# Tables of powers made per half block beside the feed-forward part, d h kept on chip by rows of W1 units, and pools on two stacks

## The chip, the cores and the metric

The kernel runs on one core of one Trainium2 chip. The time is the device time of one execution in microseconds (us); quoted times are medians of several executions. Engines are named as the profile names them: PE (matmul), PEld (PE's weight loads), DVE (vector), ACT (scalar, with activation functions), POOL (GpSimd), SP (the queue that issues most DMAs). "Clock" is the mean share of full speed that the throttle granted PE.

## The reference

A state-space layer and a feed-forward layer, forward and backward, L = 2048 positions, D = 512 channels, N = 128 states, F = 1792 hidden units, bf16. Cut to what matters:

```python
def _A_ref(u, A_re, A_im, B_re, B_im, C_re, C_im, log_dt, Dskip):
    dt = jnp.exp(log_dt)[:, None]
    logdA = dt * (A_re + 1j * A_im)
    P = jnp.exp(logdA[:, :, None] * l[None, None, :])        # powers, D x N x L
    K = jnp.einsum("dn,dnl,dn->dl", Cc, P, dt * Bc).real     # the convolution's kernel
    y = irfft(rfft(pad(u)) * rfft(pad(K)))[:L]               # by FFT
    return y + u * Dskip
def _B_ref(x, w1, w2):
    return silu(x @ w1) @ w2
xn  = layernorm(x)
out = x + _A_ref(xn, ...) * silu(_B_ref(xn, w1, w2))
# returned: out and the gradients of x, A, B, C, log_dt, Dskip, w1, w2
```

The powers P are never stored. Each power of exp(dt A) is a product of one entry of a "high" and one of a "low" table; the tables are small, and outer products on DVE expand them. The 512 channels are done in 4 blocks of 128 channels, or 8 half blocks.

## The kernel before

The order of work, in one function:

```python
    half = gen_half(k)                        # tables of powers, 4 blocks, to DRAM (k.hd)
    ...
    interleave([half, gf], [1, 2])            # gf = gen_ffn_fwd(k): beside the feed-forward part
    run(gf)
    ...
        run(gen_ssm_fwd(k, 0))                # powers of block 0, with nothing beside them
        for b in range(1, NB):
            interleave([gen_ssm_fwd(k, b), gen_conv(k, b - 1)], [1, 2])
        run(gen_conv(k, NB - 1))
    with ... pools of the backward part:
        run(gen_dw2(k))                                        # with nothing beside it
        interleave([gen_ffn_bwd(k), gen_ssm_bwd(k)], [1, 2])   # d h and d x by chunks of 512 positions
        run(gen_dw1(k))
    with tc.tile_pool(name="fin", bufs=1) as k.fin:
        run(gen_ssm_final(k))                                  # gradients of A, B, C, log_dt
```

The end of a block's tables (`gen_half`, cut): scattered products on DVE, copies on POOL, and the store.

```python
        for c in range(2):
            tmul(nc, vXL[:, :, c, :, 1:8], sp(MG[:, 10:17]), sp(RC[:, c, 10:17]))
            ...
        for h in range(2):
            nc.gpsimd.tensor_copy(out=vXH[:, h, 0:2, :, :, 1], in_=vXH[:, h, 0:2, :, :, 0])        # L453
            nc.gpsimd.tensor_copy(out=vYL[...].rearrange(...), in_=vYL[...].rearrange(...))        # L454
            yh = T4[:, h, OYH:HSZ].rearrange("p (a u) -> p a u", u=2)
            nc.gpsimd.tensor_copy(out=yh[:, :, 1], in_=yh[:, :, 0])                                # L456
            nc.gpsimd.tensor_scalar(out=T4[:, h, OXH + 2048:OYL], in0=..., scalar1=-1.0, ...)      # L457
        nc.sync.dma_start(k.hd[:, 2 * b:2 * b + 2, :], T4[:])
```

The powers (`gen_ssm_fwd`, cut). X and YY are expanded tables. KF, a block's convolution kernel, is copied out of PSUM by ACT in an order that writes single bf16 elements 128 bytes apart.

```python
            for m, (ch, cl) in enumerate(((0, 0), (2, 1), (0, 1), (1, 0))):
                outer_mul(nc, X[:, m]..., H, ...)                        # DVE, four per step
            ...                                                          # pf_t: PE turns X; ACT evicts XTf
            ps = psum.tile([P, QCH, 2, 32], F32, name="ps_k", tag="ps")
            ...                                                          # ps_k: PE
            for e in range(2):
                es = slice(64 * e, 64 * e + 64)
                k.ev_k(KF[es, :, qb:qb + QCH].rearrange("p j q -> p q j"), ps[es, :, e, :])
```

In the backward part d h is computed in chunks of 512 positions, stored to DRAM as `dht_d`, and loaded again by 14 transposing DMAs for dW1:

```python
    nc.sync.dma_start(dhv[:, :, ls], dhT[:])                             # gen_ffn_bwd, once per chunk
    ...
    nc.sync.dma_start_transpose(out=DH[:, j], in_=k.dht_d[(f0 + j) * P:(f0 + j + 1) * P, :])   # gen_dw1
```

And the last line of the final part writes the gradient of log_dt, 512 bf16 values:

```python
        nc.sync.dma_start(k.outs[8].rearrange("(k p) -> p k", p=P), ddt_b[:])
```

Of the kernel before, what the change touches and what calls it, by code (L numbers as in the profile page):

```python
# [9 lines left out]
ALU = mybir.AluOpType  # L10
# [4 lines left out]
P = 128  # L15
# [136 lines left out]
def kernel(ctx, tc, A_u, A_A_re, A_A_im, A_B_re, A_B_im, A_C_re, A_C_im, A_log_dt, A_Dskip, B_x, B_w1, B_w2, grad_out,  # L152
# [6 lines left out]
    assert L == 2048 and N == 128 and D == 512 and F % P == 0  # L159
# [6 lines left out]
    k.const = ctx.enter_context(tc.tile_pool(name="const", bufs=1))  # L166
# [8 lines left out]
    k.xt_d = dr.tile([P, D // 2, 2, P], BF16, name="xt_d")  # L175
    k.yt_d = dr.tile([P, D // 4, 2, P], BF16, name="yt_d")
    k.hd = dr.tile([P, 2 * NB, HSZ], BF16, name="hd")
    k.s_d = dr.tile([NB, P, 512], F32, name="s_d")
    k.at_d = dr.tile([F, L], BF16, name="at_d")
    k.ut_d = dr.tile([F, L], BF16, name="ut_d")  # L180
    k.dht_d = dr.tile([F, L], BF16, name="dht_d")
    k.ident = make_identity(nc, k.const)
    k.xn = k.const.tile([P, T, D], BF16, name="xn")
    k.ev_c = Evac(nc, 0); k.ev_xt = Evac(nc, 0); k.ev_yt = Evac(nc, 0); k.ev_k = Evac(nc, 0); k.ev_w = Evac(nc, 2); k.ev_v = Evac(nc, 0)
    k.ev_x = Evac(nc, 2)

    with tc.tile_pool(name="lnp", bufs=1) as k.lnp:
        k.x_sb = k.lnp.tile([P, T, D], BF16, name="x_sb")
        for t0 in range(0, T, 4):
            nc.scalar.dma_start(k.x_sb[:, t0:t0 + 4, :], k.x_v[:, t0:t0 + 4, :])  # L190
        phase_setup(k)
        phase_ln(k)
    half = gen_half(k)
    hs = ExitStack()
    k.half = hs.enter_context(tc.tile_pool(name="half", bufs=1))
    next(half)

    k.fs = ExitStack()
    k.fp = k.fs.enter_context(tc.tile_pool(name="ffnf", bufs=1))
    load_ffn(k)  # L200
    gf = gen_ffn_fwd(k)
    interleave([half, gf], [1, 2])
    run(gf)
    k.fs.close()
    hs.close()
    k.K_b = {}
    with tc.tile_pool(name="kpool", bufs=2) as k.kpool, tc.tile_pool(name="cbig", bufs=1) as k.cbig, \
            tc.tile_pool(name="cio", bufs=1) as k.cio, tc.tile_pool(name="ssmf", bufs=2) as k.sp:
        k.K_ready = lambda b: None
        run(gen_ssm_fwd(k, 0))  # L210
        for b in range(1, NB):
            interleave([gen_ssm_fwd(k, b), gen_conv(k, b - 1)], [1, 2])
        run(gen_conv(k, NB - 1))
    with tc.tile_pool(name="ssmb", bufs=2) as k.bp, tc.tile_pool(name="ffnb", bufs=1) as k.fb:
        run(gen_dw2(k))
        interleave([gen_ffn_bwd(k), gen_ssm_bwd(k)], [1, 2])
        run(gen_dw1(k))
    with tc.tile_pool(name="fin", bufs=1) as k.fin:
        run(gen_ssm_final(k))


def load_ffn(k):
# [7 lines left out]
    for t0 in range(0, T, 4):  # L230
        for dk in range(0, DK, 2):
            pt = k.psumT.tile([P, 2, 4, P], BF16, name="pt_x", tag="pt")
            for i in range(2):
                for j in range(4):
                    nc.tensor.transpose(out=pt[:, i, j, :], in_=k.xn[:, t0 + j, (dk + i) * P:(dk + i + 1) * P], identity=k.ident[:])
            k.ev_x(k.XNT[:, dk:dk + 2, t0:t0 + 4, :], pt[:])


def phase_setup(k):
# [5 lines left out]
    k.ecst = const.tile([P, 24], F32, name="ecst")  # L245
    for m, e in enumerate(HEXPS):
        nc.gpsimd.memset(k.ecst[:, m:m + 1], e / (2.0 * math.pi))
    k.ones = const.tile([P, 1], BF16, name="ones"); nc.vector.memset(k.ones[:], 1.0)
    with k.tc.tile_pool(name="setup", bufs=1) as wk:
# [11 lines left out]
        TF = const.tile([P, 16, 2, P], BF16, name="TF")  # L261
# [3 lines left out]
        TI = const.tile([P, 16, 2, P], BF16, name="TI")  # L265
# [75 lines left out]

def phase_ln(k):
# [19 lines left out]

HEXPS = [1, 2, 3, 4, 5, 6, 7, 8, 16, 24] + [32 * i for i in range(1, 8)] + [256 * i for i in range(1, 8)]

OXL, OXH, OYL, OYH, HSZ = 0, 1024, 4096, 6144, 8192


def gen_half(k):

    nc, hp = k.nc, k.half  # L370
    D = k.D
    nat = {}
    for nm, key in (("Ar", "A_A_re"), ("Ai", "A_A_im"), ("Br", "A_B_re"), ("Bi", "A_B_im"), ("Cr", "A_C_re"), ("Ci", "A_C_im")):
        nat[nm] = hp.tile([P, 1, D], BF16, name="par_" + nm)
        nc.sync.dma_start_transpose(out=nat[nm][:], in_=k.ins[key])
    ldt = hp.tile([P, D], BF16, name="ldt")
    nc.sync.dma_start(ldt[:], k.ins["A_log_dt"].unsqueeze(0).to_broadcast([P, D]))
    T4 = hp.tile([P, 2, HSZ], BF16, name="T4")
    vXL = T4[:, :, OXL:OXH].rearrange("p h (c r l) -> p h c r l", c=2, l=8)
    vXH = T4[:, :, OXH:OYL].rearrange("p h (c r l u) -> p h c r l u", c=3, l=8, u=2)  # L380
    vYL = T4[:, :, OYL:OYH].rearrange("p h (c g y r l) -> p h c g y r l", c=2, y=2, r=4, l=8)
    vYH = T4[:, :, OYH:HSZ].rearrange("p h (c g y r m u) -> p h c g y r m u", c=2, y=2, r=4, m=4, u=2)
    for c in range(2):
        v = 1.0 - c
        nc.gpsimd.memset(vXL[:, :, c, :, 0], v)
        nc.gpsimd.memset(vXH[:, :, c, :, 0, 0], v)
        for h in range(2):
            nc.gpsimd.memset(vYL[:, h, c, :, 0, :, 0], v)
            nc.gpsimd.memset(vYH[:, h, c, :, 0, :, 0, 0], v)

    pr = lambda t: t.rearrange("p (b e q) -> p b q e", e=2, q=64)
    po = lambda t: t.rearrange("p (b q e) -> p b q e", e=2, q=64)
    scr = hp.tile([P, 6, D], F32, name="scr", tag="RC")
    dtb = hp.tile([P, D], BF16, name="dtb")
    nc.scalar.activation(out=dtb[:], in_=ldt[:], func=ACT.Exp)
    lamr = hp.tile([P, D], F32, name="lamr"); tau = hp.tile([P, D], F32, name="tau")
    Ctr = hp.tile([P, D], F32, name="Ctr"); Cti = hp.tile([P, D], F32, name="Cti")
    N_ = lambda nm: nat[nm][:, 0, :]
    nc.vector.tensor_tensor(out=po(lamr[:]), in0=pr(dtb[:]), in1=pr(N_("Ar")), op=ALU.mult)
    nc.vector.tensor_tensor(out=po(tau[:]), in0=pr(dtb[:]), in1=pr(N_("Ai")), op=ALU.mult)  # L400
# [5 lines left out]
    nc.vector.tensor_tensor(out=po(Ctr[:]), in0=pr(t1), in1=pr(t2), op=ALU.subtract)  # L406
    tmul(nc, t1, N_("Cr"), dBi)
    tmul(nc, t2, N_("Ci"), dBr)
    nc.vector.tensor_tensor(out=po(Cti[:]), in0=pr(t1), in1=pr(t2), op=ALU.add)
    yield  # L410
    for b in range(NB):
        ws = slice(b * P, b * P + P)
        MG = hp.tile([P, 24, P], F32, name="MG", tag="MG")
        RC = hp.tile([P, 2, 24, P], F32, name="RC", tag="RC")
        for m, e in enumerate(HEXPS):
            nc.scalar.activation(out=MG[:, m], in_=lamr[:, ws], func=ACT.Exp, scale=float(e))
        sh = [P, 24, P]
        tmul(nc, RC[:, 1], tau[:, ws].unsqueeze(1).to_broadcast(sh), k.ecst[:].unsqueeze(2).to_broadcast(sh))
        nc.vector.tensor_scalar(out=RC[:, 0], in0=RC[:, 1], scalar1=MAGIC, scalar2=MAGIC, op0=ALU.add, op1=ALU.subtract)
        nc.vector.tensor_tensor(out=RC[:, 1], in0=RC[:, 1], in1=RC[:, 0], op=ALU.subtract)  # L420
        yield
        nc.scalar.activation(out=RC[:, 0], in_=RC[:, 1], func=ACT.Abs)
        nc.scalar.activation(out=RC[:, 0], in_=RC[:, 0], func=ACT.Sin, scale=-2.0 * math.pi, bias=k.hpi[:])
        nc.scalar.activation(out=RC[:, 1, 0:10], in_=RC[:, 1, 0:10], func=ACT.Sin, scale=2.0 * math.pi)
        nc.scalar.activation(out=RC[:, 1, 10:24], in_=RC[:, 1, 10:24], func=ACT.Sin, scale=-2.0 * math.pi)
        yield
        sp = lambda t: t.rearrange("p m (h r) -> p h r m", h=2)
        for c in range(2):
            tmul(nc, vXL[:, :, c, :, 1:8], sp(MG[:, 10:17]), sp(RC[:, c, 10:17]))
            tmul(nc, vXH[:, :, c, :, 1:8, 0], sp(MG[:, 17:24]), sp(RC[:, c, 17:24]))  # L430
            for h in range(2):
                sy = lambda t: t[:, :, 64 * h:64 * h + 64].rearrange("p m (g r) -> p g r m", r=4)
                tmul(nc, vYL[:, h, c, :, 0, :, 1:8], sy(MG[:, 0:7]), sy(RC[:, c, 0:7]))
            tmul(nc, RC[:, c, 7:10], MG[:, 7:10], RC[:, c, 7:10])
        yield
        cb = lambda t: t[:, ws].unsqueeze(1).to_broadcast([P, 3, P])
        F = lambda c: RC[:, c, 7:10]
        g1, g2, Gr, Gi = RC[:, 0, 0:3], RC[:, 1, 0:3], RC[:, 0, 3:6], RC[:, 1, 3:6]
        tmul(nc, g1, F(0), cb(Ctr))
        tmul(nc, g2, F(1), cb(Cti))  # L440
        nc.vector.tensor_tensor(out=Gr, in0=g1, in1=g2, op=ALU.subtract)
        tmul(nc, g1, F(0), cb(Cti))
        tmul(nc, g2, F(1), cb(Ctr))
        nc.vector.tensor_tensor(out=Gi, in0=g1, in1=g2, op=ALU.add)
        for h in range(2):
            sy = lambda t: t[:, :, 64 * h:64 * h + 64].rearrange("p m (g r) -> p g r m", r=4)
            s1 = lambda t: t[:, b * P + 64 * h:b * P + 64 * h + 64].rearrange("p (g r) -> p g r", r=4)
            for c, (G_, C_) in enumerate(((Gr, Ctr), (Gi, Cti))):
                nc.scalar.copy(out=vYH[:, h, c, :, 0, :, 1:4, 0], in_=sy(F(c)))
                nc.scalar.copy(out=vYH[:, h, c, :, 1, :, 1:4, 0], in_=sy(G_))  # L450
# [413 lines left out]
```

## Time and profile before

The time was 1192.91 us, the median of 3 executions (1191.68 to 1198.79); a fourth, beside the first run of the changed kernel, makes the median 1195.09. The profiled execution spans 1186.1 us at a mean clock of 0.835.

Busy time of each engine over the whole span (part 1 of the page before), with the share of the span and the number of instructions:

```profile
PE 775.2 (65%) x6033; PEld 459.1 (39%) x6033; DVE 744.3 (63%) x1126; ACT 650.0 (55%) x1091; POOL 136.7 (12%) x96
```

No engine is near full, so the averages tell nothing of what to change. The windows view divides the span into stretches. Columns: from and to, the length, busy us of each engine with its number of instructions, the granted clock, the busy share of the DMA engines, GB/s. The cuts are at events of the program: the first feed-forward matmul (30), the first powers (310), the end of convolution 2 (695) and of convolution 3 (763), the first d h matmul (858), a cut in the last dW1 work (1109), after the last matmul (1171; the row of the last 15 us, without work on any engine, is left out).

```profile
core 0: us, PE busy (x) PEld busy (x) DVE busy (x) ACT busy (x) POOL busy (x), PEclk, DMA share, GB/s
0.00:30.00 30.00, 5.08 (x51) 4.37 (x52) 24.43 (x87) 13.66 (x13) 9.66 (x49) 1.00 0.62 201
30.00:310.00 280.00, 131.29 (x512) 50.77 (x511) 210.54 (x244) 160.50 (x319) 120.03 (x46) 0.73 0.40 145
310.00:695.00 385.00, 286.61 (x3612) 234.03 (x3613) 280.97 (x431) 330.82 (x500) 0.00 (x0) 0.86 0.48 150
695.00:763.00 68.00, 48.79 (x424) 34.02 (x421) 27.83 (x37) 52.54 (x93) 0.78 (x1) 0.87 0.19 47
763.00:858.00 95.00, 55.78 (x221) 22.47 (x222) 8.55 (x8) 4.09 (x7) 6.23 (x2) 0.82 0.97 222
858.00:1109.00 251.00, 196.75 (x965) 87.95 (x963) 162.61 (x271) 81.06 (x148) 0.00 (x0) 0.88 0.82 222
1109.00:1171.00 62.00, 50.91 (x256) 25.44 (x256) 29.35 (x48) 7.32 (x13) 0.00 (x0) 0.91 0.76 170
...
```

Read it by rows. In 30:310 (feed-forward and tables) PE is busy 131 of 280 us, and even DVE only 75%: engines wait for each other. In 310:695 (powers and convolutions 0 to 2) ACT is busy 331 of 385 us, 86%: it sets the pace. In 763:858 (dW2) DMA is busy 0.97 of the time and all engines are idle for much of it.

Who waited for whom in the feed-forward stretch, in the waits view of 30 to 310 (waiter <- what it waited for: us in total, number of times, longest):

```profile
POOL T_370 L454 <- DVE T_370 L60: 82.2, 3, 40.6
PE ps_h L478 <- ACT th L482: 76.8, 10, 35.5
DVE T_370 L60 <- DMA hd<-T_370: 38.2, 2, 22.9
...
ACT T_370 L449 <- DMA hd<-T_370: 21.3, 1, 21.3
```

PE waited 76.8 us for ACT to take its results out of PSUM, and in single waits of up to 35.5 us, far longer than any ACT instruction there. During that longest wait (167.3 to 202.8 us in the timeline) ACT stood for 21.3 us before a table instruction (L449), and the evictions that PE waited for ran only after it. So there is a chain from block to block: POOL waits for DVE, DVE and ACT wait for the store of the previous block's tables, and that store waits for POOL's copies, as the waits of the SP queue show:

```profile
SPq L458 <- POOL T_370 L456: 57.1, 4, 27.5
```

What those copies cost, from the groups of POOL (busy us, mean ns of one):

```profile
L454 POOL COPY T_370<-T_370 128x1024 bf16<-128x1024 bf16 x8 | 62.7, 7841 | 82.2 <-DVE T_370 L60 82.2
L457 POOL TENSOR_SCALAR T_370<-T_370 128x1024 bf16<-128x1024 bf16 x8 | 23.6, 2963 | 0.0
L453 POOL COPY T_370<-T_370 128x1024 bf16<-128x1024 bf16 x8 | 17.7, 2248 | 28.4 <-DVE T_370 L60 28.4
L456 POOL COPY T_370<-T_370 128x1024 bf16<-128x1024 bf16 x8 | 11.2, 1440 | 1.6 <-ACT T_370 L450 1.6
```

And two groups of part 5 of the page before: the KF eviction, with 1321 ns for 64x256 elements where 128x512 elements take 621, and one form of the feed-forward matmul.

```profile
L478 PE MATMUL ps_h<-XNT,W_403 128*128 128x512 bf16 x224 | 67.0, 451 | 102.9 <-ACT th L482 76.8
...
L74 ACT CAST KF<-ps_k 64x256 bf16<-64x256 f32 x64 | 84.6, 1321 | 4.1 <-PE ps_k L564 3.6
...
L74 ACT CAST XTf<-pf_t 128x512 bf16<-128x512 f32 x128 | 67.4, 621 | 17.3 <-PE pf_t L540 17.1
```

### The profile page before, as it was taken

How to read it: one execution, taken by the hardware profiler on the slowest of the kernel's cores; microseconds unless marked ns; L12 is line 12 of the kernel's file. 1: busy time of each engine (PE TensorE's matmuls, PEld its weight loads, DVE VectorE, ACT ScalarE, POOL GpSimd, SP SyncE). 2: the span in 40 equal slices, each digit the busy share in tenths (PEclk: the TensorE clock that was granted, in tenths of full speed). 3: DMA queues.
4: the chain of work that ended last, by engine and by line, in shares of the span. 5: the costliest groups of instructions: out<-in, count | busy, mean ns of one | idle time of the engine just before them, and what ended most of it. 6: DMA issues, size and time to landing. Idle time of an engine off the chain costs nothing. (4 is left out here: it accounts for less than half of the span.)

```text
span 1186.1 us, 15777 instructions
## 1 busy us (share of the span) xinstructions
PE 775.2 (65%) x6033; PEld 459.1 (39%) x6033; DVE 744.3 (63%) x1126; ACT 650.0 (55%) x1091; POOL 136.7 (12%) x96
## 2 busy tenths in 40 slices
PE   1462261367477777877777777546896886867693
PEld 1220020123266656656665654412342342423242
DVE  8788665896687759857965914600076575756153
ACT  4787362745177997999799797400042332323110
POOL 3229294360000000000000000200000000000000
PEclk9896675778777988899899888778998988988697
DMA  6221506538764513841651350499876889788981
GB/s 204 59 83 46 205 21 257 212 113 306 259 212 158 178 55 120 219 151 72 159 188 54 119 123 1 114 247 203 203 240 183 236 230 245 225 221 216 204 185 47
DMA packets 273262, 194.90 MB, mean 164 GB/s; under 512 B 189666, under 2 KB 250979, under 8 KB 271651
## 3 DMA queue, kind: packets, MB, share of 16 engines
q1 hardware_dynamic: 271842, 188.13, 55.0%
q0 software_dynamic: 768, 3.67, 0.9%
q10 hardware_dynamic: 576, 2.10, 0.6%
q8 instruction: 47, 0.77, 0.3%
q14 instruction: 29, 0.23, 0.1%
HBM read 84.28 MB, written 86.25 MB: 144 GB/s over the span
## 5 line engine op out<-in xcount | busy, mean ns | idle before, releaser
L74 ACT CAST Vb<-psV 128x512 bf16<-128x512 f32 x128 | 67.5, 595 | 124.5 <-PE psV L737 84.9
L478 PE MATMUL ps_h<-XNT,W_403 128*128 128x512 bf16 x224 | 67.0, 451 | 102.9 <-ACT th L482 76.8
L519 DVE TENSOR_TENSOR X<-H 128x1024 bf16<-128x1024 bf16 x128 | 83.8, 689 | 74.5 <-PE ps_k L564 64.6
L540 PE MATMUL pf_t<-ident_bfloat_80,X 128*128 128x128 bf16 x1024 | 93.8, 254 | 49.7 <-ACT KF L74 27.3
L540 PEld LDWEIGHTS <-X 128*128 128x128 bf16 x1024 | 80.3, 116 | 60.7 <-issue 52.6
L74 ACT CAST KF<-ps_k 64x256 bf16<-64x256 f32 x64 | 84.6, 1321 | 4.1 <-PE ps_k L564 3.6
L478 PEld LDWEIGHTS <-W_403 128*128 128x128 bf16 x224 | 23.7, 109 | 160.9 <-issue 144.4
L74 ACT CAST XTf<-pf_t 128x512 bf16<-128x512 f32 x128 | 67.4, 621 | 17.3 <-PE pf_t L540 17.1
L60 DVE TENSOR_TENSOR T_370<-MG,RC 128x896 bf16<-128x896 f32 (+1 forms) x32 | 49.2, 1615 | 43.0 <-DMA hd<-T_370 38.2
L737 PE MATMUL psV<-XT,Gbd 128*128 128x256 bf16 x256 | 48.1, 323 | 40.5 <-DMA XT<-xt_d 40.2
L454 POOL COPY T_370<-T_370 128x1024 bf16<-128x1024 bf16 x8 | 62.7, 7841 | 82.2 <-DVE T_370 L60 82.2
L713 POOL MEMSET Gbd<- 64x4096 bf16 x2 | 7.0, 3505 | 493.9 <-PE ps_i_7911 L130 493.9
L495 PE MATMUL ps_o<-W_405,aT 128*128 128x512 bf16 x224 | 57.2, 415 | 5.2 <-ACT th L482 5.2
L737 PEld LDWEIGHTS <-Gbd 128*128 128x128 bf16 x256 | 34.5, 178 | 64.9 <-DMA XT<-xt_d 30.4
L662 PE MATMUL ps_da<-DOT,W2T 128*128 128x512 bf16 x224 | 57.1, 400 | 0.2
L674 PE MATMUL ps_dx<-W1T,dhT 128*128 128x512 bf16 x224 | 56.3, 408 | 0.0
L632 PEld LDWEIGHTS <-A_ft 128*128 128x128 bf16 x224 | 22.7, 105 | 73.9 <-DMA A_ft<-at_d 28.7
L74 ACT COPY dftB<-pt_b 128x1024 bf16<-128x1024 bf16 x48 | 46.2, 1054 | 3.4 <-PE pt_b L95 3.3
L564 PE MATMUL ps_k<-YY,X 128*128 128x64 bf16 x1024 | 42.7, 203 | 7.1 <-ACT KF L74 6.6
L564 PEld LDWEIGHTS <-X 128*128 128x128 bf16 x1024 | 40.7, 105 | 9.8 <-issue 8.6
L95 PE MATMUL pt_b<-ident_bfloat_80,dftA 128*128 128x128 bf16 x384 | 31.8, 236 | 17.9 <-ACT dftB L74 10.7
L74 ACT COPY YTf<-pt_t 128x1024 bf16<-128x1024 bf16 x32 | 34.6, 1080 | 13.6 <-issue 8.5
(1576 smaller groups left out, 1932.3 us busy)
## 6 DMA issues: line engine op xcount, KB each, us to landing
hd<-T_370 SPq DMA_DIRECT2D x4, 4096.0 KB, 11.9
H<-hd SPq DMA_DIRECT2D x8, 2048.0 KB, 9.1
xt_d<-XTf SPq DMA_DIRECT2D x32, 512.0 KB, 3.1
XT<-xt_d SPq DMA_DIRECT2D x32, 512.0 KB, 4.5
YT<-yt_d SPq DMA_DIRECT2D x128, 128.0 KB, 4.5
yt_d<-YTf SPq DMA_DIRECT2D x32, 256.0 KB, 2.0
ut_d<-u SPq DMA_DIRECT2D x28, 256.0 KB, 2.4
at_d<-aT SPq DMA_DIRECT2D x4, 1792.0 KB, 6.8
```

The lines of the kernel that those rows point to most:

```text
L60: nc.vector.tensor_tensor(out=out, in0=a, in1=b, op=ALU.mult)
L74: self.nc.scalar.copy(out=out, in_=in_)
L95: nc.tensor.transpose(out=pt[:, gi, :], in_=A[:, c, g0 + gi, :, :].rearrange("p t e -> p (t e)"), identity=k.ident[:])
L454: nc.gpsimd.tensor_copy(out=vYL[:, h, :, :, 1].rearrange("p c g r l -> p c g (r l)"), in_=vYL[:, h, :, :, 0].rearrange("p c g r l -> p c g ...
L478: nc.tensor.matmul(out=ps[:], lhsT=W1[:, dk, ft * P:(ft + 1) * P], rhs=XNT[:, dk, 4 * tcn:4 * tcn + 4, :], start=(dk == 0), stop=(dk == DK ...
L495: nc.tensor.matmul(out=pso[:], lhsT=aT[:, ft, tt * P:(tt + 1) * P], rhs=W2[:, ft, :], start=(ft == 0), stop=(ft == FT - 1))
L519: nc.vector.tensor_tensor(out=out.rearrange("p (r h l u) -> p r h l u", h=nh, l=4, u=2), in0=h, in1=l, op=ALU.mult)
L540: nc.tensor.matmul(out=pf[:, qi, m // 2, :], lhsT=X[:, m, q + qi], rhs=k.ident[:], start=(m % 2 == 0), stop=(m % 2 == 1))
L564: nc.tensor.matmul(out=ps[:, q].rearrange("p e j -> p (e j)"), lhsT=X[:, m, q], rhs=YY[:, m // 2, q // 2, 1, 64 * (q % 2):64 * (q % 2) + 6 ...
L662: nc.tensor.matmul(out=ps[:], lhsT=W2T[:, dk, ft * P:(ft + 1) * P], rhs=DOT[:, dk, ls], start=(dk == 0), stop=(dk == DK - 1))
L674: nc.tensor.matmul(out=ps[:], lhsT=dhT[:, ft, tt * P:(tt + 1) * P], rhs=W1T[:, ft, :], start=(ft == 0), stop=(ft == FT - 1))
L737: nc.tensor.matmul(out=psV[:, qi].rearrange("p a b -> p (a b)"), lhsT=Gbd[:, :, :, :, 32 * (q_ // 2 % 2) + 4 * c + 2 * (q_ % 2) + q_ // 4] ...
```

## The change

The intent has four parts.

- **Tables on chip, per half block.** `half_angles` and `half_tables` make the tables of one half block (64 channels) in SBUF, right before they are used. The round trip through DRAM goes, POOL's copies go (a broadcast in the DVE product writes both copies), and 24 small Exps of a block become one for each half block.
- **Powers beside the feed-forward part.** `gen_ssm_fwd` is one generator for all half blocks, and 42 of its steps are issued between the steps of the feed-forward part. KF is evicted in an order that writes runs of eight elements.
- **Backward by rows of W1 units.** `gen_dh` takes 128 hidden units at a time, keeps d h in SBUF, turns it on PE, and does dW1 at once. d x comes last, with the last block's state-space backward (`gen_ssm_bwd`) and the final part, now in two parts (blocks 0 to 2, then block 3), beside it.
- **Pools.** Pools stand on two stacks ("left", "right") and release memory tile by tile, so that stages can overlap.

```diff
+    def pool(name, side, bufs=1):
+        return tc.tile_pool(name=name, bufs=bufs, side=side, reuse_waits="tile")
...
-    half = gen_half(k)
...
-    interleave([half, gf], [1, 2])
-    run(gf)
...
-        run(gen_ssm_fwd(k, 0))
-        for b in range(1, NB):
-            interleave([gen_ssm_fwd(k, b), gen_conv(k, b - 1)], [1, 2])
-        run(gen_conv(k, NB - 1))
-    with ... as k.bp, ... as k.fb:
-        run(gen_dw2(k))
-        interleave([gen_ffn_bwd(k), gen_ssm_bwd(k)], [1, 2])
-        run(gen_dw1(k))
-    with tc.tile_pool(name="fin", bufs=1) as k.fin:
-        run(gen_ssm_final(k))
+    gs = gen_ssm_fwd(k)
+    with pool("ffnf", "right") as k.fp:
+        load_ffn(k)
+        interleave([gen_ffn_fwd(k), BoundedGen(gs, 42)], [1, 1])
+    ...
+    for b in range(NB - 1):
+        upto(b)
+        interleave([BoundedGen(gs, 26), gen_conv(k, b)], [1, 2])
+    upto(NB - 1)
+    run(gs)
+    ...
+    gd = gen_dw2(k); gb = chain([gen_ssm_bwd(k, b) for b in range(NB - 1)])
+    interleave([gen_conv(k, NB - 1), BoundedGen(gb, 24)], [2, 1])
+    next(gd)
+    ...
+        with pool("ffnb", "right") as k.fb:
+            interleave([chain([gd, gen_dh(k)]), gb], [2, 1])
+        def final():
+            yield from gen_ssm_bwd(k, NB - 1)
+            for b0, nb in ((0, NB - 1), (NB - 1, 1)):
+                with pool("fin", "left") as k.fin:
+                    yield from gen_ssm_final(k, b0, nb)
+        with pool("dxp", "right", 2) as k.dp:
+            interleave([gen_dx(k), final()], [1, 3])
...
+def half_tables(k, w0):
+    tmul(nc, vXL[:, 0:2, :, 1:8], mg(10, 17), rc(10, 17))
+    for c in range(2):
+        tmul(nc, vXH[:, c, :, 1:8, :], mg(17, 24)[:, 0].unsqueeze(3).to_broadcast([P, 64, 7, 2]), rc(17, 24)[:, c]....)
...
-                k.ev_k(KF[es, :, qb:qb + QCH].rearrange("p j q -> p q j"), ps[es, :, e, :])
+                k.ev(KF[es, :, ql:ql + QCH], ps[es, :, e, :].rearrange("p q j -> p j q"))
+            if ql == 0 and hb + 1 < 2 * NB:
+                half_angles(k, 64 * (hb + 1))
...
+def gen_dh(k):
+    for ft in range(FT):
+        ...                                          # ps_da: PE; d h to k.dhT (SBUF): DVE
+            for j in range(8):
+                nc.tensor.transpose(out=pt[:, j, :], in_=k.dhT[:, ft, (t0 + j) * P:(t0 + j + 1) * P], identity=k.ident[:])
+            k.ev(DH[:, t0:t0 + 8, :], pt[:])
+        for t in range(T):
+            nc.tensor.matmul(out=ps[:], lhsT=DH[:, t, :], rhs=k.xn[:, t, :], start=(t == 0), stop=(t == T - 1))
```

## The prediction

> **What bounds the kernel now.** No single engine. The page gives PE 775 us, DVE 744, ACT 650 of a span of 1186. Busy times by stretch (windows view):
>
> | us | work | PE | DVE | ACT | POOL | DMA |
> |---|---|---|---|---|---|---|
> | 38-310 | FFN forward, tables | 125 | 204 | 156 | 118 | 0.41 |
> | 396-690 | powers 1-3, conv 0-2 | 224 | 214 | 268 | 0 | 0.43 |
> | 762-858 | dW2 | 56 | 9 | 5 | 7 | 0.96 |
> | 858-1105 | dh, dx, SSM backward | 195 | 160 | 81 | 0 | 0.82 |
> | 1105-1186 | dW1, final | 53 | 32 | 8 | 0 | 0.63 |
>
> The first is latency-bound (waits: PE 103 us on ACT; DVE 38 us on the table store; POOL copies of 7.8 us), the third ACT-bound, dW2 DMA-bound (A_ft transposes).
>
> **Removed.** The table round trip through DRAM (32 of 195 MB); 118 us of POOL; 96 small Exps (20 us of ACT) for 8 large ones; the d h round trip with 14 DMA transposes. YT loads: 128 become 64, in 2 KB runs.
>
> **Added.** Tables come in half width with more strided DVE work: about 18 us per half block (estimate from 2.08 us per 128x896 product), 148 us against 111. PE: 224 transposes of d h, 56 of dW1, about 31 us. ACT: 28 evictions of 1.05 us and, by the instruction order, 20 table loads against 14, 1.28 us each.
>
> **ACT.** KF evictions write single elements 128 B apart and took 1.31 us for 64x256. The Trainium skill, "ScalarE: Activation LUTs" (What ACT_TABLE_LOAD costs), gives 186 ns + 0.833 ns per element, so 0.40 us; 128x512 evictions (0.60) agree. The new order writes runs of eight but reads PSUM strided; I estimate 0.6 us: 64 x 0.7 = 45 us of ACT less. Totals: ACT about 647, DVE 785, PE 806.
>
> **New stages, from the busiest engine.**
> - Setup with parameters and first tables: 38 becomes 50.
> - FFN forward + 3.1 of 8 half blocks: ACT 200, PE 190, DVE 186; at 85%, 235.
> - conv 0-2 + 4.9 half blocks: ACT 280, DVE 277, PE 200; at 88%, 315.
> - conv 3 + SSM backward 0: PE 75, ACT 68: 80.
> - dW2, dh, dW1 + SSM backward 1-2: PE 56+57+53+31+40 = 238; about 255. DMA moves 43 MB, not limiting.
> - dx + SSM backward 3 + final: PE 76; 95 with the tail.
>
> Sum 1030; overlap across stages (pools released tile by tile) may give 15 back. About 170 us come off the critical path: 75 before conv 3, 95 after, where DMA-bound dW2 and dW1 get PE work beside them.
>
> **Predicted: 1015 us, 8 in 10 within 950 to 1080.** Faster by over 2%: 0.94; within 2%: 0.04; slower: 0.02.
>
> **Shown right by:** POOL near 20 us; about 150 MB moved; KF eviction at or below 0.7 us; FFN stretch with PE over 75%; conv stretch with DVE and ACT over 80%; no stretch with DMA over 0.9 and PE under 0.6. **Wrong** if KF stays at 1.3 us, or PE is below 85% in the d h stretch.
>
> **What would make it wrong.** In-order ACT, now fed by silu, evictions and tables, may stall the others: then the first two stretches run at 70% (1080). One buffer for T4, PC and DH may serialize halves.

## More of the kernel before

The mean of L454 hides two kinds. In POOL's timeline the first copy made for each of the four blocks is a long one: 22.2, 26.8 and 7.6 us (L454) and 7.0 us (L453). The other five copies of L454 took 1.03 to 1.43 us. Two of them, of one block (start us, us):

```profile
141.53 26.79 POOL L454 COPY T_370<-T_370 128x1024 bf16<-128x1024 bf16 x1 [23.97 <-DVE T_370 L60]
...
171.06 1.04 POOL L454 COPY T_370<-T_370 128x1024 bf16<-128x1024 bf16 x1
```

So the same copy need not take long on POOL. DVE was busy for over 99% of each long one (26.63 of 26.80 us in the one shown), but throughout some of the short ones too (1.26 and 1.03 us), so what held the long ones up is not shown. PE's wait of 35.5 us began as the copy of 26.79 us ended.

## The result, and the profile after

The changed kernel took **1029.72 us**, the median of 4 executions (1026.76 to 1033.08). Its ratio to the kernel before is 0.8617, with a 95% interval of 0.8576 to 0.8657. Here and below a ratio is the mean time of one kernel's fast runs over that of the other's of the same rounds, so it is not quite the ratio of the medians that are quoted. The profiled execution spans 1031.3 us at a clock of 0.894.

Part 1 of the page after:

```profile
PE 731.1 (71%) x6215; PEld 444.3 (43%) x6281; DVE 735.1 (71%) x1196; ACT 619.0 (60%) x1062; POOL 20.7 (2%) x85
```

PE's count is 66 below PEld's: some matmul records are missing from this trace, so that PE's busy time is a little too low. The windows view after, with the same columns and cuts at the same events (first feed-forward matmul 60, end of the feed-forward part 238, end of convolution 2 at 543 and of convolution 3 at 625, first d h matmul 710, first d x matmul 886, last matmul 970):

```profile
0.00:60.00 60.00, 11.79 (x98) 10.37 (x100) 48.17 (x126) 27.05 (x28) 13.67 (x83) 0.85 0.40 103
60.00:238.00 178.00, 149.64 (x1326) 85.54 (x1348) 162.31 (x261) 152.10 (x273) 0.00 (x0) 0.95 0.59 188
238.00:543.00 305.00, 222.01 (x2723) 174.59 (x2734) 258.40 (x375) 265.50 (x468) 7.01 (x2) 0.89 0.47 114
543.00:625.00 82.00, 61.81 (x540) 39.26 (x541) 48.22 (x63) 67.64 (x125) 0.00 (x0) 0.98 0.76 180
625.00:710.00 85.00, 60.62 (x255) 25.80 (x262) 15.40 (x18) 8.21 (x15) 0.00 (x0) 0.86 0.93 209
710.00:886.00 176.00, 151.89 (x924) 76.20 (x936) 107.82 (x135) 64.45 (x98) 0.00 (x0) 0.95 0.60 170
886.00:970.00 84.00, 73.37 (x355) 32.57 (x362) 65.99 (x137) 29.99 (x53) 0.00 (x0) 0.95 0.67 187
970.00:1031.00 61.00, 0.00 (x0) 0.00 (x0) 28.75 (x85) 4.05 (x7) 0.00 (x0) 0.53 0.12 28
```

Row against row, the two tables give where the time went (lengths in us, from the two windows views):

| stretch | before | after | difference |
|---|---|---|---|
| setup | 30 | 60 | +30 |
| feed-forward, tables; after: with about 3 of 8 half blocks of powers | 280 | 178 | -102 |
| the (other) powers, convolutions 0 to 2 | 385 | 305 | -80 |
| convolution 3 (after: with state-space backward 0) | 68 | 82 | +14 |
| dW2 | 95 | 85 | -10 |
| d h, d x, dW1, the rest of the state-space backward | 251 + 62 | 176 + 84 | -53 |
| after the last matmul | 15 | 61 | +46 |

So the front half, to the end of convolution 2, gave 152 us, and the back half only 3. Inside the back half 49 us were gained before the last matmul and 46 lost after it.

The waits of PE in the feed-forward stretch, in the waits view of 60 to 238 after, answer to those shown of before:

```profile
PE pf_t L532 <- ACT th L594: 6.0, 8, 2.0
...
PE ps_h L590 <- ACT th L594: 1.5, 4, 0.4
```

The long waits are gone: PE waits for ACT by 2.0 us at most where one wait had lasted 35.5. The feed-forward matmul in part 5 of the page after, and the KF eviction among ACT's groups by shape after:

```profile
L590 PE MATMUL ps_h<-XNT,W_408 128*128 128x512 bf16 x210 | 53.1, 389 | 2.6 <-ACT th L594 1.5
```

```profile
L74 ACT CAST KF<-ps_k 64x256 bf16<-64x256 f32 x64 | 24.9, 389 | 1.0 <-PE ps_k L556 0.5
```

KF went from 1321 to 389 ns. The feed-forward matmul went from 451 to 389 ns in the mean though nothing in it was changed. Its median is 380 ns before and 379 after, and single ones took up to 635; the granted clock of its stretch was 0.73 before and 0.95 after.

The end of the span after, in the timeline of the SP queue (start us, us, what is issued):

```profile
986.26 0.37 SPq L884 DMA_DIRECT2D out_dram<-ddt_b_10739  x1
...
989.58 4.00 SPq L822 DMA_DIRECT2D n_ldt_10758<-in_A_log_dt_dram  x1
999.98 1.73 SPq L850 DMA_DIRECT2D S_10803<-s_d  x4
...
1013.54 0.38 SPq L884 DMA_DIRECT2D out_dram<-ddt_b_10908  x1
```

The queue issues the first final part's write of 2-byte elements at 986.26, and the parameter loads of the second right behind it. The second part's state sums (S) are issued only at 999.98. The last write is issued at 1013.54, and the span ends at 1031.3. What these gaps were is in the chain of waits (start, us, link) of 970 to 1031, where the longest link is the first of these writes, and in the waits of the SP queue:

```profile
986.26 13.70 DMA out_dram<-ddt_b_10739
```

```profile
SPq L909 <- DMA out_dram<-ddt_b_10908: 16.1, 1, 16.1
...
SPq L850 <- DMA out_dram<-ddt_b_10739: 6.4, 1, 6.4
```

Of the 61 us, 13.7 went to a write of 768 bytes on which the loads of S waited, and 16.1 to one of 256 bytes at the very end.

### The profile page after: what moved, and what is told of

Its sections match the earlier page's. It is cut to its first block, busy times and chain, and to the rows that moved or that the text cites. A ratio compares the mean times of both kernels' runs of the same rounds, so it can differ in the third digit from the quotient of the medians.

```text
span 1031.3 us, 16058 instructions
## 1 busy us (share of the span) xinstructions
PE 731.1 (71%) x6215; PEld 444.3 (43%) x6281; DVE 735.1 (71%) x1196; ACT 619.0 (60%) x1062; POOL 20.7 (2%) x85
## 5 line engine op out<-in xcount | busy, mean ns | idle before, releaser
L506 DVE TENSOR_TENSOR X<-T_511 128x1024 bf16<-128x1024 bf16 x128 | 84.4, 704 | 14.7 <-PE ps_k L556 14.7
L532 PE MATMUL pf_t<-ident_bfloat_78,X 128*128 128x128 bf16 x1024 | 76.6, 230 | 22.9 <-DVE X L506 8.6
L532 PEld LDWEIGHTS <-X 128*128 128x128 bf16 x1024 | 67.9, 104 | 33.3 <-issue 17.2
L590 PE MATMUL ps_h<-XNT,W_408 128*128 128x512 bf16 x210 | 53.1, 389 | 2.6 <-ACT th L594 1.5
L60 DVE TENSOR_TENSOR T_511<-PC 128x896 bf16<-128x896 f32 (+1 forms) x40 | 51.7, 1348 | 0.4 <-ACT PC L452 0.4
L74 ACT COPY DH<-pt_dh 128x1024 bf16<-128x1024 bf16 x28 | 27.9, 1033 | 37.0 <-PE pt_dh L712 36.9
L680 PEld LDWEIGHTS <-A_ft 128*128 128x128 bf16 x224 | 23.0, 106 | 59.6 <-DMA A_ft<-at_d 30.1
L706 DVE SCALAR_TENSOR_TENSOR dhT<-th_ft,ps_da 128x512 bf16<-128x512 bf16 x56 | 35.6, 682 | 8.4 <-PE ps_da L705 8.2
L556 PEld LDWEIGHTS <-X 128*128 128x128 bf16 x1024 | 35.9, 100 | 6.1 <-issue 1.5
L87 PEld LDWEIGHTS <-TF 128*128 128x128 bf16 x384 | 28.1, 106 | 23.1 <-issue 21.7
L594 ACT ACTIVATE th<-ps_h 128x512 bf16<-128x512 f32 x56 | 37.8, 675 | 0.0
L593 ACT ACTIVATE aT<-ps_h 128x512 bf16<-128x512 f32 x56 | 37.4, 669 | 0.5 <-PE pf_t L532 0.3
```

Of the source, the lines that this page charges most:

```text
L60: nc.vector.tensor_tensor(out=out, in0=a, in1=b, op=ALU.mult)
L74: self.nc.scalar.copy(out=out, in_=in_)
L506: nc.vector.tensor_tensor(out=out.rearrange("p (r h l u) -> p r h l u", h=nh, l=4, u=2), in0=h, in1=l, op=ALU.mult)
L532: nc.tensor.matmul(out=pf[:, qi, m // 2, :], lhsT=X[:, m, q + qi], rhs=k.ident[:], start=(m % 2 == 0), stop=(m % 2 == 1))
L556: nc.tensor.matmul(out=ps[:, q].rearrange("p e j -> p (e j)"), lhsT=X[:, m, q], rhs=YY[:, m // 2, q // 2, 1, 64 * (q % 2):64 * (q % 2) + 6 ...
L590: nc.tensor.matmul(out=ps[:], lhsT=W1[:, dk, ft * P:(ft + 1) * P], rhs=XNT[:, dk, 4 * tcn:4 * tcn + 4, :], start=(dk == 0), stop=(dk == DK ...
```

## The experiments

All twelve kernels gave correct results. The eight named t1 to t4 and f1 to f4 ran on one chip, where the kernel before had a median of 1197.5 us, the four named e1 to e4 on another, where it took 1194.7 us. The changed kernel itself was timed in neither group, so differences against its 1029.72 us may cross chips; the ratio to the kernel before, from the same chip in each case, is the safer number and is given each time. The changed kernel's ratio is 0.8617.

### Front half: is it the overlap?

Theory OVERLAP: the 152 us of the front half come from powers that now run beside the feed-forward part. Rival TABLES: they come from cheaper tables, whatever runs beside them. f1 keeps the new tables and runs the 42 steps after the feed-forward part.

```diff
-        interleave([gen_ffn_fwd(k), BoundedGen(gs, 42)], [1, 1])
+        run(gen_ffn_fwd(k))
+        run(BoundedGen(gs, 42))
```

> Changed kernel with the feed-forward forward run to its end first, and the same 42 steps of powers and tables after it. In the changed kernel both together took 178 us (60 to 238) at PE 150, DVE 162, ACT 152 busy. Theory OVERLAP: the gain ahead of conv 3 (152 us, where 75 were predicted) comes from running the two beside each other. Alone, the FFN takes about 120 us (PE 107 us busy) and three half blocks at DVE 43 us each about 135: 255 together, so the run takes 65 to 85 us more, 1095 to 1115. Rival TABLES: it is the new making of tables (no POOL, no store to DRAM) that freed the FFN; then running apart costs under 35 us, below 1065.

Measured: 1072.24 us, ratio 0.8954 (0.8933 to 0.8976), so 43 us more than the changed kernel. This lies between the two theories. The windows view of f1, feed-forward part and then the 42 steps:

```profile
60.00:172.00 112.00, 105.73 (x485) 45.10 (x493) 60.74 (x115) 84.39 (x157) 0.00 (x0) 1.00 0.63 207
172.00:268.00 96.00, 55.28 (x834) 48.79 (x830) 95.68 (x142) 66.01 (x112) 0.00 (x0) 0.74 0.46 130
```

Alone, the feed-forward part is bound by PE (106 of 112 us, clock 1.00), and the powers are bound by DVE (95.7 of 96 us). They need different engines, and so they fit into one another: 208 us apart, 178 together, 30 us; by the end of convolution 2 f1 is 40 us behind. (The profiled execution of f1 was its slowest, 1081.66 us and so 9 above its median, so these two are a little high.) The two parts were not wholly apart even here, since the first half block was ready 19 us after the feed-forward part and each further one took 38.4 us. So overlap is worth 43 us and, as an estimate from these two numbers, at most some 19 more: between 28% and 41% of the 152.

### Front half: the KF eviction

Theory ACT: where ACT sets the pace, the 0.93 us saved in each of 64 KF evictions come off the time. Rival: other engines fill the gap. f2 puts the old order into the changed kernel, f3 the new order alone into the kernel before.

```diff
 (f2, in the kernel after)
-                k.ev(KF[es, :, ql:ql + QCH], ps[es, :, e, :].rearrange("p q j -> p j q"))
+                k.ev(KF[es, :, ql:ql + QCH].rearrange("p j q -> p q j"), ps[es, :, e, :])
 (f3, in the kernel before)
-                k.ev_k(KF[es, :, qb:qb + QCH].rearrange("p j q -> p q j"), ps[es, :, e, :])
+                k.ev_k(KF[es, :, qb:qb + QCH], ps[es, :, e, :].rearrange("p q j -> p j q"))
```

> Changed kernel with the KF evictions written as before, single elements 64 B apart, instead of runs of eight. They take 0.39 us each now and took 1.32 before: 60 us of ACT more over 64. Theory ACT: ACT is 265 of 305 us busy in the conv stretch and 152 of 178 in the FFN stretch, so it becomes the limit of both: 35 to 55 us more, 1065 to 1085. Rival SLACK: DVE (258 of 305, 162 of 178) sets the pace and ACT fills its gaps: at most 15 us more.

> The kernel before with only the order of the KF eviction changed. ACT was 331 of 385 us busy from 310 to 695. Theory ACT: 60 us of ACT less there; the next limits are PE 287 and DVE 281, so 35 to 55 us less: 1140 to 1160. Rival SLACK: under 15 us less.

Measured: f2 1076.07 us, ratio 0.8976 (0.8937 to 0.9015), 46 us more than the changed kernel. f3 1146.74 us, ratio 0.9586 (0.9554 to 0.9618), 51 us less than before on the same chip. The KF groups of f2 and of f3:

```profile
L74 ACT CAST KF<-ps_k 64x256 bf16<-64x256 f32 x64 | 83.7, 1307 | 0.5
```

```profile
L74 ACT CAST KF<-ps_k 64x256 bf16<-64x256 f32 x64 | 24.8, 387 | 2.1 <-PE ps_k L564 1.7
```

One line is worth 46 to 51 us in either kernel, against 59 us of ACT time saved (83.7 - 24.9): theory ACT holds. The duration itself agrees with the Trainium skill, "ScalarE: Activation LUTs" (What ACT_TABLE_LOAD costs): 186 ns + 0.833 ns x 256 is 399 ns, and the traces show 387 and 389. That the old order costs 3.4 times as much fits the note on 16-byte cachelines in "SBUF — State Buffer" (Door 1: The DMA port swizzle), by which each access that crosses to a new line pays a penalty: the old order wrote every element 128 bytes from the last (64 in f2, whose KF tile is half as wide), the new one runs of eight bf16, 16 bytes. The runs show the two durations; that the cacheline is the reason was not tested: the edit changes the order of the reads from PSUM together with that of the writes.

### Front half: the copies on POOL

Theory POOL: in the kernel before, POOL's copies stood in the chain of the tables and so in front of ACT and PE. Rival: moved to DVE, the busiest engine of the stretch, they cost as much there. f4 moves the four copies, nothing else, in the kernel before.

```diff
-            nc.gpsimd.tensor_copy(out=vXH[:, h, 0:2, :, :, 1], in_=vXH[:, h, 0:2, :, :, 0])
+            nc.vector.tensor_copy(out=vXH[:, h, 0:2, :, :, 1], in_=vXH[:, h, 0:2, :, :, 0])
 (the other three alike)
```

> The kernel before with the copies of the tables on DVE instead of POOL. The FFN stretch took 280 us; POOL was 118 us busy in it with copies of 7.8 us, DVE 204. On DVE the copies should cost about 25 us (an estimate from 0.7 us for 1024 elements written whole[...]). Theory POOL: the tables wait for POOL and with them the store, DVE and the in-order ACT; the stretch gets 30 to 60 us shorter, 1135 to 1165 us. Rival CHAIN: the stretch is held by ACT and DVE waiting on each other and on the store of one table tile with a single buffer, which stays: within 15 us of 1195.

Measured: 1153.3 us, ratio 0.9629 (0.9608 to 0.9651), 44 us less than before. Groups of DVE in f4:

```profile
L60 DVE TENSOR_TENSOR T<-MG,RC 128x896 bf16<-128x896 f32 x16 | 32.9, 2055 | 7.5 <-ACT RC L423 7.5
...
L454 DVE COPY T<-T 128x1024 bf16<-128x1024 bf16 x8 | 3.3, 415 | 0.0
```

On DVE all four copies cost 18.4 us together, on POOL 115 us (62.7 + 23.6 + 17.7 + 11.2): the copy of L454 takes 415 ns on DVE; on POOL it took 7841 in the mean and 1384 in the median. The feed-forward stretch shrank from 280 to 237 us, in the windows view of f4:

```profile
30.00:267.00 237.00, 137.07 (x501) 52.44 (x508) 204.22 (x276) 160.14 (x319) 5.57 (x13) 0.76 0.47 171
```

Theory POOL holds: the copies' place on POOL cost the time. Why the first copy of each block took so long on POOL, f4 cannot tell, since it takes all of them away. The first line of DVE's groups settles a side question: the product of 128x896 takes 2055 ns without POOL, as before with it (2081), so its 1471 ns in the changed kernel comes from the new layout and not from a quiet POOL.

Together: KF 46 to 51, POOL 44, overlap 43 are 133 to 138 of the 152 us. The three need not add exactly, each being measured in a kernel of its own. The rest, some 15, is the sum of several untested terms: no table round trip through DRAM, fewer small Exps, and against them 30 us of later start.

### Back half: what does the end of the span wait for?

Two theories for the tail. MEMORY: the second final part's loads of S go into memory that the first part's tiles still hold, and these are held until the 13.7 us write of ddt_b has landed. LOADS: the second part waits for its own parameter loads (ACT waited 12.6 us for n_ldt, DVE then 12.1 for ACT), which are issued too late. t1 loads the parameters of both parts early, into a pool of their own; t2 leaves the loads and has PE turn ddt_b, so that the write is in rows.

```diff
 (t1)
+            with pool("finp", "left") as fpar:
+                par = {b0: load_final(k, b0, nb, fpar) for b0, nb in ((0, NB - 1), (NB - 1, 1))}
                 yield from gen_ssm_bwd(k, NB - 1)
...
+                        yield from gen_ssm_final(k, b0, nb, par[b0])
 (t2)
-        nc.sync.dma_start(k.outs[8][bs].rearrange("(k p) -> p k", p=P), ddt_b[:])
+    pt = k.psumT.tile([DK, P], BF16, name="pt_ddt", tag="pt")
+    nc.tensor.transpose(out=pt[:], in_=ddt_b[:], identity=k.ident[:])
+    row = fin.tile([DK, P], BF16, name="ddt_row" + sfx)
+    nc.vector.tensor_copy(out=row[:], in_=pt[:])
+    nc.sync.dma_start(k.outs[8][bs].rearrange("(k p) -> k p", p=P), row[:])
```

> Changed kernel with the parameter loads of both final parts made early, in a pool of their own. Changed kernel: 1029.7 us. Theory LOADS: the 12.1 us that DVE waited before the second final part are the late parameter loads (put into the queue at 986.7, log dt landed at about 1000), so this run ends 10 to 13 us earlier, about 1018. Theory MEMORY: the loads of S for block 3 wait anyway until the slow write of the first ddt (986.3 to 1000.0) has left the memory that they reuse, so only the products of parameters (2 us) come off: 1025 to 1029. Theory DVE: DVE is 97% busy from 960 to 990 and sets the end; 1025 or later.

> Changed kernel with both ddt results turned into rows by PE before they are written (256 B runs instead of single 2-byte elements); nothing else. MEMORY: the first write no longer holds the reload of S (12 us), and the last write takes 2 us instead of 16: together 24 to 28 us less, 1002 to 1006. LOADS: only the last write shrinks, 14 us: about 1016. DVE: at most 14 us too.

Measured: t1 1027.74 us, ratio 0.8588 (0.8555 to 0.8621): 2 us, inside the noise. The S loads still came late, and the SP queue still waited for the write before them; the waits views of t1 from 960 on:

```profile
DVE cm L60 <- DMA S<-s_d: 11.6, 2, 9.2
...
SPq L860 <- DMA out_dram<-ddt_b: 9.0, 1, 9.0
```

t2 1009.47 us, ratio 0.8421 (0.8397 to 0.8445): 20 us less. Here S is loaded right behind the parameters, in the timeline of the SP queue of t2:

```profile
994.05 7.69 SPq L850 DMA_DIRECT2D S<-s_d  x16
```

MEMORY holds, and LOADS falls as the main cause: with the parameters early nothing was won, with the write short 20 us were. But most of the 20 is the last write, which LOADS allowed too: from its issue to the end of the span 17.8 us became 2.4. The first write's part is the smaller one, since the last is issued only 5.5 us sooner (1008.03 against 1013.54); MEMORY had put the whole at 24 to 28. What sets the pace there in t2, by its chain of waits, is the SP queue, which issues the parameter and S loads one by one from 990.5 to 1001.7 us. The late parameters were in part the write's doing as well: the load of log_dt's last 128 elements, issued right behind the write, held ACT up for 12.6 us in the changed kernel and for 4.4 in t2. "DMA: Bandwidth & Descriptors" (Specifications) gives 512 bytes as the least transfer at line rate and a read-modify-write below that. This does not tell the two writes apart: the rows of t2 have 256 bytes, and the last landed within 2.4 us. The traces show 13.7 us for 384 single elements and 16.1 for 128; why they take so long was not tested.

t3 does all of it: rows, parameters early, and the final part of blocks 0 to 2 ahead of the last state-space backward, so that only block 3 is left at the end.

```diff
                 with pool("fin", "left") as k.fin:
-                    yield from gen_ssm_final(k, b0, nb)
+                    yield from gen_ssm_final(k, 0, NB - 1, par[0])
+                yield from gen_ssm_bwd(k, NB - 1)
+                with pool("fin", "left") as k.fin:
+                    yield from gen_ssm_final(k, NB - 1, 1, par[NB - 1])
```

> Rows for ddt, parameters early, and the final part of blocks 0 to 2 put ahead of the backward of block 3, so that only the small final part of block 3 is left after it. If the tail is latency of a chain that could run beside d x, the end comes near the end of the d x work on DVE (989): 990 to 998 us, 33 to 40 us less than the changed kernel. Theory DVE: moving it only crowds DVE in the d x stretch; no better than the run with rows alone (over 1003).

Measured: 994.66 us, ratio 0.831 (0.8291 to 0.8329): 35 us less than the changed kernel and 15 less than rows alone; how the 15 divide between the early parameters (2 us by themselves, in t1) and the new order was not separated. The stretch from the first d x matmul to the end went from 145 to 108 us, against 95 in the prediction.

### Back half: dW2 and d h

dW2 was to have PE work beside it. In the changed kernel d h follows dW2 in one chain, and only the state-space backward is beside it: PE is busy 61 us of 85, 5 us more than in the dW2 stretch before, with DMA at 0.93. t4 runs two steps of dW2 and then the rest of it between steps of d h.

```diff
-            interleave([chain([gd, gen_dh(k)]), gb], [2, 1])
+            next(gd); next(gd)
+            interleave([gd, gen_dh(k), gb], [1, 3, 3])
```

> Changed kernel, but after two dW2 steps the rest of dW2 runs mixed with the d h steps instead of ahead of them. Theory DMA: the dW2 stretch (85 us, DMA share 0.93, PE 61 us busy, 30 us of waits for A_ft) is bound by the transposing loads; spread over the 261 us of both stretches (PE 212 busy) they hide, and the run takes 15 to 25 us less: 1005 to 1015. Rival ORDER: the in-order queue of loads delays a_ft, th_ft and XT behind the transposes as much as it hides; within 8 us of 1029.7.

Measured: 994.56 us, ratio 0.8305 (0.8279 to 0.8332): 35 us less, more than expected. dW2, d h and dW1 together took 224 us instead of 261; the windows view of t4:

```profile
622.00:700.00 78.00, 61.78 (x340) 29.43 (x348) 35.11 (x41) 17.60 (x27) 0.00 (x0) 0.93 0.95 241
700.00:846.00 146.00, 139.13 (x833) 70.41 (x846) 87.75 (x111) 54.00 (x86) 0.00 (x0) 0.98 0.75 195
```

The second stretch has PE busy 95% of the time. The transposing loads are no fewer, but PE has other matmuls to do while they run.

e1 asks what keeping d h on chip is worth: it stores d h row by row to DRAM and loads it by transposing DMAs, as before, in place of the turns on PE. For room, two output tiles had one buffer instead of two, so a little of its loss may be theirs.

```diff
-            for j in range(8):
-                nc.tensor.transpose(out=pt[:, j, :], in_=k.dhT[:, ft, (t0 + j) * P:(t0 + j + 1) * P], identity=k.ident[:])
-            k.ev(DH[:, t0:t0 + 8, :], pt[:])
+        nc.sync.dma_start(k.dht_d[rows, :], k.dhT[:, ft, :])
+        DH = fb.tile([P, T, P], BF16, name="DH", tag="DH", bufs=2)
+        nc.sync.dma_start_transpose(out=DH[:], in_=k.dht_d[rows, :])
 (dW1 of row ft is done one row later; ob and wt get bufs=1)
```

> Changed kernel with d h brought back into row order as before, by a store to DRAM and a transposing load for each row tile, instead of 16 transposes on PE and two evictions on ACT; the product with xn is delayed by one tile, and two output tiles have one buffer instead of two for room. Theory DMA: 14 more transposing loads and 14 MB more traffic in a stretch with DMA at 0.60, behind the dW2 stretch at 0.93, make it DMA-bound: 10 to 40 us more, 1040 to 1070. Rival PE: the stretch is PE-bound (152 of 176 us), the transposes are 19 us of it, and the loads hide: 10 to 20 us less, 1010 to 1020.

Measured: 1043.98 us, ratio 0.8751 (0.8718 to 0.8784): 14 us more, at the low end of what the DMA theory expected. The d h stretch has DMA at 0.91 instead of 0.60. From PE's waits in e1, from 625 to 895:

```profile
PE ps_w L698 <- DMA DH<-dht_d: 28.2, 8, 6.4
```

PE waits 28 us for the loads that replace its own turns: d h on chip pays, by a good deal less than the two weak places of the back half cost.

### Pools released tile by tile

e2 takes `reuse_waits="tile"` out of the pools.

```diff
-        return tc.tile_pool(name=name, bufs=bufs, side=side, reuse_waits="tile")
+        return tc.tile_pool(name=name, bufs=bufs, side=side)
```

> Changed kernel without the release of pools tile by tile: a pool that reuses memory waits for the whole of the pool before it. The prediction gave it 15 us. Theory EDGE: at four changes of stage (setup to FFN, FFN to conv, powers and conv to backward, d h to d x) the first loads and tiles wait for the last reader: 10 to 25 us more, 1040 to 1055. Rival NONE: first users are in program order behind the last readers anyway; within 6 us.

Measured: 1037.58 us, ratio 0.8697 (0.8669 to 0.8725): 8 us more (by the ratios 10), where the prediction had put 15 on it; this lies between the two theories. In its profile convolution 2 ends at 544.8 and convolution 3 at 625.7 us, about 2 us later than in the changed kernel, and the profiled span is 1032.9 against 1031.3. But these are the fastest of its executions and the slowest of the changed kernel's, so the two profiles can't show where the 8 us arise. It was not found, and since the changed kernel may have run on another chip, part of them may be the chip's.

### The version that beats both

e3 is t3 and t4 together; if they act in different places, their gains add.

> Changed kernel with the tail moved (rows for ddt, parameters early, first final part ahead) and dW2 spread over d h. The two gains, 35 us each, are in different stretches and should add: 955 to 965 us. If the d x stretch was held by DVE, which the earlier start does not change, or the tail's extra work meets the same loads: 970 to 985.

Measured: **957.02 us**, the median of 6 executions (952.85 to 963.4), ratio 0.8026 (0.7995 to 0.8057), so 73 us less than the changed kernel: 35 + 35, and the gains add. From its windows view, the stretch of dW2, d h and dW1 and that at the end:

```profile
622.00:850.00 228.00, 207.00 (x1202) 101.14 (x1202) 123.39 (x154) 74.33 (x116) 0.00 (x0) 0.96 0.83 210
...
930.00:961.00 31.00, 20.11 (x93) 8.34 (x91) 27.76 (x84) 6.77 (x10) 0.00 (x0) 0.90 0.23 79
```

PE is busy 207 of 228 us (91%) in the first, and in the last 31 us DVE works for 27.8 (the last d x matmul is at 950).

e4 takes up the setup, 60 us instead of 30, where DVE is busy 48 of 60: it prepares the state-space parameters after the layer norm instead of ahead of it.

```diff
-        ssm_prep(k)
         phase_setup(k)
         phase_ln(k)
+        ssm_prep(k)
```

> The run with both, with the preparation of the parameters put behind the layer norm instead of ahead of it. PE has no FFN work before 59 us, where the kernel before started it at 31. Theory START: the FFN starts 8 to 15 us earlier and the end comes 6 to 15 us earlier. Rival DVE: DVE is 162 of 178 us busy in the FFN stretch and 48 of 60 before it, so the same work is only moved behind; within 5 us.

Measured: 959.72 us, ratio 0.8039 (0.8013 to 0.8065): no gain over e3. The feed-forward part starts at 53.5 instead of 58.7 us, but convolution 2 ends at 544.5 instead of 541.7. The same DVE work only moves: to the end of convolution 2 DVE is busy 468 us in both, and the feed-forward stretch that takes it over has DVE busy 90% of the time in e4.

## Why the prediction was right and wrong

The total was right: 1015 us were predicted, 950 to 1080 as the range, and 1029.7 were measured. It was right in part because errors cancelled.

| stage as predicted | predicted | measured |
|---|---|---|
| setup | 50 | 60 |
| feed-forward + 3.1 half blocks | 235 | 178 |
| convolutions 0 to 2 + 4.9 half blocks | 315 | 305 |
| convolution 3 + state-space backward 0 | 80 | 82 |
| dW2, d h, dW1 | 255 | 261 |
| d x + state-space backward 3 + final | 95 | 145 |
| sum | 1030 | 1031 |

**Right in mechanism.** POOL is at 20.7 us and 154 MB are moved (194.9 before). KF is at 0.39 us. The conv stretch has ACT at 87% and DVE at 85%; the feed-forward stretch has PE at 84%, and the d h stretch 86%. The totals of busy time were all put too high (PE 806, measured 731; DVE 785, 735; ACT 647, 619). f2, f3 and f4 show that KF and POOL's copies stood on the critical path; e1 shows that a d h round trip costs 14 us when it is put back into the changed kernel. The 15 us given to pools measured some 8 to 10.

**The step that failed: "About 170 us come off the critical path: 75 before conv 3, 95 after."** Measured, 152 came off before conv 3 and 3 after. The prediction's own stages do not give 75 and 95 either: 50 + 235 + 315 is 95 below the 695 us at which convolution 2 ended before, and 80 + 255 + 95 is 61 below the remaining 491. The two terms at fault are these.

- *The feed-forward stretch, "at 85%, 235", measured 178.* All three busy times in it were put too high: PE 190 (measured 150, some records missing), ACT 200 (152), DVE 186 (162). PE's was built on 125 us read at a clock of 0.72; at a clock of 1.00 the feed-forward part takes 106 (f1), which is 19 of the 40 us, and its matmul fell from 451 to 389 ns between the two kernels. "TensorE: Matmul & The Clock Gate" (What's actually happening) says that the throttled clock is the default and that activity releases it, and the feed-forward stretches agree: with PE busy 47% of it before, the clock was 0.73, with 84% after 0.95, with 94% in f1 1.00. The share alone does not fix the clock, though: the first 30 us before have PE busy 17% at 1.00, and after, 73% and 75% go with 0.89 and 0.98. ACT's sum was too high by KF at 0.6 in place of 0.39 and DVE's by products of 1.47 us in place of 2.08, but these two explain only about 5 of 48 us (24 evictions) and 6 of 24 (9 products); the rest of both was not worked out. And the stretch ran at 91% of its busiest engine, not at 85%.
- *"dx + SSM backward 3 + final: PE 76; 95 with the tail", measured 145.* PE's 73 us in 84 were about right; what was missed is that the final part, split in two, puts its slow write of 2-byte elements twice in line, once ahead of the loads of the second half. The profile before had shown the cost, 16.0 us from issue to landing for this very write, but then it was paid once. t2 and t3 show the place: 20 and 35 us of it come back.
- The setup was 10 us too low.

**The sentence that half held: "where DMA-bound dW2 and dW1 get PE work beside them".** The sign set for it (no stretch with DMA over 0.9 and PE under 0.6) held to the letter, at 0.93 and 0.71, but dW2 stayed bound by DMA: PE's loads of weights waited 30.1 us for its transposed tiles against 28.7 before. The stage sums nearly fit, 261 against 255, again by two errors: PE's work was put at 238 us and measured 213 (60.6 + 151.9), and PE was to be busy 93% of the stretch and was 81%. t4 shows that 35 us more were there.

**What stays open.** About 15 of the front half's 152 us were not tested one by one, e2's 8 us were not located, and why the first of POOL's copies for each block took so long is not shown.

## What to carry to other kernels

Take a busy time from a stretch together with the clock that was granted there: the feed-forward part's PE time, read at 0.72 as 125 us, was 106 at 1.00. When a change splits an ending in two, look at every slow DMA of that ending, at what may not start before it has landed, and at whether it is now paid twice. And check a right total stage by stage: here errors of -57 and +50 us hid one another, and the second was 35 us to be had.

## What the Trainium skill lacked or had wrong

- "ScalarE: Activation LUTs" (What ACT_TABLE_LOAD costs) gives 186 ns + 0.833 ns per element, with no term for how the output lies. For 64x256 elements that is 399 ns; runs of eight bf16 took 387 to 389 ns, single elements 64 bytes apart 1307 (f2) and 128 bytes apart 1321 (before). "SBUF — State Buffer" names a penalty for each new 16-byte line, without a number.
- The same note in "SBUF — State Buffer" says that any non-contiguous PSUM access slows matmuls, and no page says what it does to ACT's reads. The new KF eviction reads PSUM at strides of 256 bytes and takes 389 ns, no more than the 399 of the formula above.
- "DMA: Bandwidth & Descriptors" has no duration for writes of single 2-byte elements: 384 took 13.7 us, 128 took 16.1 and 512 took 16.0, while a read of 512 such elements took 4.0 and the write in rows landed within 2.4 us (issued at 1008.03, span 1010.4, in t2).
- "GPSIMD Engine Reference" (4.1 Engine selection) calls one-input elementwise work on GpSimd roughly line-rate, without a figure. Four forms of it on 128x1024 bf16 took 1364, 1384, 1628 and 3000 ns there in the median, and 415 to 747 ns in the mean on DVE. The five short copies of L454 (1.03 to 1.43 us for 1024 elements) do not contradict the page; the mean of 7841 ns comes from three copies of 7.6 to 26.8 us, whose cause is open.
